# Moving one Q/K piece and the batched output rows inside a recurrent segment loop

## The chip, the cores and the metric

The kernel runs on one core of a Trainium2 chip. The metric is the device time of one execution in microseconds.

## The reference

Part A is a recurrent attention layer: 64 segments of 32 rows, each with 8 memory rows in front. The memory of the next segment is what this segment's output projection gives for those 8 rows, so the segments form one chain. Part B, a gated MLP with a spatial mix over all 2048 rows, follows and is not touched.

```python
for s in range(n_seg):                      # 64 segments, H = 32 heads of 128, Dm = 512
    h = concat([mem, x[:, 32*s:32*s+32]])   # 8 memory rows + 32 rows
    q, k, v = h @ Wq, h @ Wk, h @ Wv        # per head
    p = softmax(where(mask, q @ k.T * scale, -1e9))
    o = einsum(p @ v, Wo)                   # 40 rows x 512
    mem = o[:, :8]                          # next segment's memory
    outs.append(o[:, 8:])
# [...] residual, layer norm, part B
```

## The kernel before

An emitter records the instructions of five engines in program order and derives from read and written tokens which semaphore each one waits for. A PSUM bank is one token: a matmul that writes a bank waits until every earlier reader of that bank on another engine is done.

A matmul has 32 weight columns (`hT`, the segment's own rows) and up to 512 moving columns; four of them stand side by side in the array as four column strips. I call these four a **round**. With `held` the weights of the previous round are kept, so no load is issued. **PV** is the product of the probabilities and V, **Wo** the output projection; the matmuls of Wo come in two **stretches**. A **hole** is a time in which TensorE would only wait for another engine.

```python
    QKP = ((0, 0, 8, 0, 0), (0, 0, 8, 1, 1), (1, 0, 8, 0, 6), (1, 0, 4, 1, 7), (1, 4, 4, 1, 2))   # (head half, first, count, 0=Q 1=K, PSUM bank)
    UBK = (0, 1)
    PVB = (0, 1, 6, 7)
    VB = {(0, 0): 6, (1, 0): 7, (1, 2): 2}
    OB = 2
    XB = 3
    # [...]
    OB2 = 6
```

```python
    def QK(s, k, dc, first=0, last=3, held=False):
        b, p0, np_, mi, bank = QKP[k]
        sl = slot(s)
        ws = (w_q, w_k)[mi]
        h0, nh = 16 * b + 2 * p0, 2 * np_
        for c in range(4):
            rhs = ws[:, dc, :].rearrange("p (h c i) -> p c h i", c=4, i=32)[:, c, h0:h0 + nh, :]
            pe(lambda e, c=c, rhs=rhs: mm(e, held, ps[32 * c:32 * c + 32, bank, 0:32 * nh], hT[:, sl, dc, :], rhs,
                                          dc == first, dc == last, (0, 32 * c)),
               reads=[("hTx", (s // 4) % 3), ("hTm", s, dc // 2), ("W", mi, 2 * b), ("W", mi, 2 * b + 1)], writes=[PB(bank)])
```

Each of the five Q/K pieces is evacuated by ScalarE (L559) and then transposed by VectorE (L567). In between it lies in the buffer `Tst`, which has a place for Q and one for K, but not one for each head half: piece 2 (Q of half 1) is written over piece 0 (Q of half 0). The scores of head half 0 need pieces 0 (Q) and 1 (K); those of half 1 need pieces 2, 3 and 4.

```python
    def QK_evac(piece):
        b, p0, np_, mi, bank = piece
        st_ = Tst[:, mi, 64 * p0:64 * (p0 + np_)]
        tok = [("T", mi, k) for k in halves(b, p0, np_)]
        act(lambda e: e.activation(out=st_.rearrange("p (hp i r) -> p hp i r", i=32, r=2),
                                   in_=ps[:, bank, 0:64 * np_].rearrange("p (hp r i) -> p hp i r", r=2, i=32), func=ACT.Copy),
    # [...] VectorE transposes Tst into QT or KT
```

The recurrence runs through `mem_out`: two halves of the memory rows are transposed by small matmuls (L722) and copied into `hT`, the first by VectorE (L728), the second by ScalarE (L730).

```python
    def mem_out(s, hf):
        bank = GB[hf]
        for dd in range(2):
        # [...] small matmuls with G_sb
        dst = hT[:, slot(s + 1), 2 * hf:2 * hf + 2, 0:M]
        src = ps[:, bank, 0:2 * M].rearrange("p (dc c) -> p dc c", c=M)
        if hf == 0:
            dve(lambda e: e.tensor_copy(out=dst, in_=src), reads=[PB(bank)], writes=[("hTm", s + 1, hf)])
        else:
            act(lambda e: e.activation(out=dst, in_=src, func=ACT.Copy), reads=[PB(bank)], writes=[("hTm", s + 1, hf)])
```

The loop body, with the cuts marked. `xs` is side work for later chunks of segments; `fill` takes batched output rows (L751 and, twice per four segments, L736 and L761) from a queue: ten rounds for each four segments.

```python
        QK(s, 0, 0)
        QK(s, 1, 0, last=2, held=True)
        if s > 0:
            mem_out(s - 1, 1)
        # [...]
        QK(s, 0, 1)
        QK(s, 1, 1, last=2, held=True)
        QK(s, 0, 2)
        QK(s, 0, 3)
        QK_evac(QKP[0])
        QK(s, 1, 3, last=2, held=True)
        QK(s, 1, 2, last=2)
        QK_evac(QKP[1])
        QK(s, 2, 2, first=2, last=0, held=True)
        QK(s, 2, 3, first=2, last=0)
        QK(s, 2, 1, first=2, last=0)
        QK(s, 2, 0, first=2, last=0)
        lastop["q"] = em.by_eng["pe"][-1]
        QK_evac(QKP[2])
        QK(s, 3, 0, held=True)
        QK(s, 4, 0, last=2, held=True)
        QK(s, 3, 1)
        QK(s, 4, 1, last=2, held=True)
        QK(s, 3, 2)
        QK(s, 3, 3)
        QK_evac(QKP[3])
        QK(s, 4, 3, last=2, held=True)
        QK(s, 4, 2, last=2)
        lastop["k"] = em.by_eng["pe"][-1]
        QK_evac(QKP[4])
        # [...]
        S_half(s, 0)
        sm_exp(0)
        for dc in range(DC):
            V_half(s, 0, (0, 4), dc)            # into bank 6
        V_evac(0, "dve")
        # [...] sums, exponentials, second scores, second half of V
        nw1, nw2, nw4 = (2, 1, 2, 1)[j4], 0, 1
        # [...]
        fill(nw1)
        for f in xs[:2]:
            f()
        PV_half(s, 0)
        PV_half(s, 1)
        for f in xs[2:4]:
            f()
        fill(nw2)
        # [...] eight evacuations of PV into cT by ScalarE and VectorE
        Wo(WOQ, OB, 0, OC)
        part_evac(s, OB, 0, OC)
        Wo(WOQ[:6], OB2, OC, D)
        if s + 1 < NSEG:
            mem_out(s, 0)
            mask_dve()
        Wo(WOQ[6:], OB2, OC, D)
        cTx_copy(s)
        part_evac(s, OB2, OC, D)
        # [...]
        fill(nw4)
```

The softmax here doesn't subtract the row's maximum and nothing guards it: scores larger than these inputs give would overflow.

Of the kernel before, what the change touches and what calls it, by code (L numbers as in the profile page):

```python
# [178 lines left out]
def fast_path(nc, st, keep, A_x, A_mem0, A_Wq, A_Wk, A_Wv, A_Wo, A_seg_len, B_w_in, B_w_sp, B_b_sp, B_w_out, out):  # L179
# [98 lines left out]
    def PB(b):  # L278
        return ("ps", b)
# [4 lines left out]
    def pe(fn, **k):  # L284
        return em.add("pe", fn, **k)

    def mm(e, hold, out, lhsT, rhs, start, stop, pos):
        if not hold:
            return e.matmul(out, lhsT=lhsT, rhs=rhs, start=start, stop=stop, skip_group_check=True, tile_position=pos)  # L289
        return e.add_instruction(mybir.InstMatmult(  # L290
            name=nc.get_next_instruction_name(), engine=mybir.EngineType.PE, ins=[e.lower_ap(rhs), e.lower_ap(lhsT)], outs=[e.lower_ap(out)],
            start_tensor_calc=start, stop_tensor_calc=stop, tile_size=(128, 32), tile_position=pos, bass_skip_group_check=True,
            ldweights=False))
# [118 lines left out]
    def slot(s):  # L412
        return s % NSLOT
# [120 lines left out]
    XB = 3  # L534
    WXB = 4
    GB = (1, 2)
    OB2 = 6
    FBK = 7
    OC = 256

# [10 lines that stand above are left out]
# [4 lines left out]
# [6 lines that stand above are left out]
            reads=[PB(bank)], writes=tok)  # L561
        src = st_.bitcast(U32)
        dt_, nm = ((QT, "QT"), (KT, "KT"))[mi]
        dst = dt_[:, b, p0:p0 + np_, :, :].rearrange("p hp q r -> p (hp q r)").bitcast(U32)
        if mi == 0:
            dst = dst.rearrange("p (hp q) -> p hp q", hp=np_)[:, :, 8:40]
        dve(lambda e: e.transpose(out=dst, in_=src), reads=tok, writes=[(nm, b, k) for k in halves(b, p0, np_)])  # L567
# [16 lines left out]
    def mask_dve():  # L584
        dve(lambda e: e.tensor_copy(out=ps[:, SB, 0:448], in_=mask[:, :]), reads=["mask"], writes=[PB(SB)])
# [110 lines left out]
    def Wo(cbs, bank, d0, d1):  # L696
        for c, b in cbs:
            for g in range(4):
                h = 16 * b + 4 * c + g
                i = 8 * c + 4 * b + g  # L700
                pe(lambda e, h=h, g=g, i=i, b=b, c=c: e.matmul(  # L701
                    ps[32 * g:32 * g + 32, bank, 0:d1 - d0], lhsT=cTh[:, i, 8:40], rhs=w_o[:, h, d0:d1], start=((c, b) == WOQ[0]),
                    stop=((c, b) == WOQ[-1]), tile_position=(0, 32 * g)),
                    reads=[("cT", c, b), ("Wo", h // 8)], writes=[PB(bank)])

    def cTx_copy(s):
        j = s % 4
        dst = cTx[:, (s // 4) % 2, :, 8 * j:8 * j + 8]
        pool(lambda e: e.tensor_copy(out=dst, in_=cTh[:, :, 0:8]), reads=[("cT", c, b) for c in range(4) for b in range(2)],
             writes=[("cTx", (s // 4) % 2)])  # L710

    def part_evac(s, bank, d0, d1):
        act(lambda e: e.activation(out=part[:, s % 8, d0:d1], in_=ps[:, bank, 0:d1 - d0], func=ACT.Copy), reads=[PB(bank)],  # L713
            writes=[("part", s % 8, d0 // OC)])
# [4 lines that stand above are left out]
            dc = 2 * hf + dd  # L719
            for c in range(4):  # L720
                c0 = dc * 128 + 32 * c
                pe(lambda e, dd=dd, c=c, c0=c0: e.matmul(ps[32 * c:32 * c + 32, bank, dd * M:(dd + 1) * M], lhsT=part[:, s % 8, c0:c0 + 32],  # L722
                                                         rhs=G_sb[:, :], start=True, stop=True, skip_group_check=True, tile_position=(0, 32 * c)),
                   reads=[("part", s % 8, hf), "G"], writes=[PB(bank)])
# [6 lines that stand above are left out]
# [16 lines left out]
    def WoX_mm(rb, qr, bgs=range(8)):  # L747
        for bg in bgs:
            b, g = bg // 4, bg % 4
            h = 16 * b + 4 * qr + g  # L750
            pe(lambda e, h=h, g=g, i=8 * qr + bg: e.matmul(ps[32 * g:32 * g + 32, WXB, :], lhsT=cTx[:, rb % 2, i, :], rhs=w_o[:, h, :],  # L751
                                                           start=(i < 4), stop=(i >= H - 4), tile_position=(0, 32 * g)),
               reads=[("cTx", rb % 2), ("Wo", h // 8)], writes=[PB(WXB)])
# [181 lines left out]
    for s in range(NSEG):  # L935
        j4 = s % 4
# [9 lines left out]

        QK(s, 0, 0)
        QK(s, 1, 0, last=2, held=True)
        if s > 0:
            mem_out(s - 1, 1)  # L950
            for f in late:
                f()
        if s == NSEG - 1:
            load_h(rb)
        QK(s, 0, 1)
        QK(s, 1, 1, last=2, held=True)
        QK(s, 0, 2)
        QK(s, 0, 3)
        QK_evac(QKP[0])
        QK(s, 1, 3, last=2, held=True)  # L960
        QK(s, 1, 2, last=2)
        QK_evac(QKP[1])
        QK(s, 2, 2, first=2, last=0, held=True)
        QK(s, 2, 3, first=2, last=0)
        QK(s, 2, 1, first=2, last=0)
        QK(s, 2, 0, first=2, last=0)
        lastop["q"] = em.by_eng["pe"][-1]
        QK_evac(QKP[2])
        QK(s, 3, 0, held=True)
        QK(s, 4, 0, last=2, held=True)  # L970
        QK(s, 3, 1)
        QK(s, 4, 1, last=2, held=True)
        QK(s, 3, 2)
        QK(s, 3, 3)
        QK_evac(QKP[3])
        QK(s, 4, 3, last=2, held=True)
        QK(s, 4, 2, last=2)
        lastop["k"] = em.by_eng["pe"][-1]
        QK_evac(QKP[4])
        if s == NSEG - 1:  # L980
# [41 lines left out]
        if j4 == 0 and rb > 0:  # L1022
            assert not wq
            wq.extend(lambda rb=rb, k=k: WoX_mm(rb - 1, k // 2, range(4 * (k % 2), 4 * (k % 2) + 4)) for k in range(8))
        nw1, nw2, nw4 = (2, 1, 2, 1)[j4], 0, 1
        if not xs:
            nw1, nw2 = 1, nw1 - 1

# [24 lines left out]
# [8 lines that stand above are left out]
        if j4 == 0 and 2 <= rb + 2 < RB:  # L1061
# [904 lines left out]
def build_kernel(nc, A_x, A_mem0, A_Wq, A_Wk, A_Wv, A_Wo, A_seg_len, B_x, B_w_in, B_w_sp, B_b_sp, B_w_out, out):  # L1966
    args = (A_x, A_mem0, A_Wq, A_Wk, A_Wv, A_Wo, A_seg_len, B_w_in, B_w_sp, B_b_sp, B_w_out, out)
    with contextlib.ExitStack() as keep:
        with contextlib.ExitStack() as st:
            em, sems, dsems, flag = fast_path(nc, st, keep, *args)  # L1970
# [88 lines left out]
```

## Time and profile before

| | before |
|---|---|
| time, median of 4 runs | 854.16 us (852.58 to 854.69) |
| span of the profiled execution | 848.4 us |
| first Q/K round of segment 1, of segment 63 | 57.55, 663.69 us |
| after that (last segment and part B) | 184.7 us |
| quiet period of a segment, odd / even | 9.721 / 9.738 us |

The **period** is the distance between the first Q/K rounds (L289) of two segments (numbered from 0), read from the timeline of TensorE. Single segments are disturbed by pauses of 0.02 to 0.8 us at changing places. I therefore give the lower quartile of the periods from the fifth segment on, odd and even segments apart, and call it the quiet period; the segments differ by parity since even ones carry three batched rows and odd ones two. (In the code odd segments are those with `j4` 1 or 3.)

In a timeline line the columns are: start in us, length in us, engine, source line, operation, output and inputs, shape, count, and in brackets the idle time before it with what ended it. For TensorE the length is a modelled latency, so a pause shows as a distance between starts that is larger than the columns need: 0.216 us for a round of 512 columns, 0.109 us for 256.

### The profile page before, as it was taken

What the parts mean: (1) busy time and instruction counts of PE and PEld (TensorE: products, weight loads), DVE (VectorE), ACT (ScalarE), POOL (GpSimd) and SP (SyncE); (2) the same over time, 40 slices, a digit from 0 to 9 for tenths busy, and PEclk for the clock granted to TensorE, in tenths of its full rate; (3) what the DMA queues carried; (4) which work ended last, traced back from release to release, by engine and by line L of the source; (5) the groups of instructions that cost most, each with busy time, mean ns of one, the idle gap of its engine ahead of it and who ended that gap; (6) DMA issues with size and microseconds to landing.
All of it is one profiled execution on the core that took longest, in us unless ns stands there. A gap on an engine that the chain in (4) does not pass through costs nothing.

```text
span 848.4 us, 46072 instructions
## 1 busy us (share of the span) xinstructions
PE 834.1 (98%) x22552; PEld 438.3 (52%) x19480; DVE 515.3 (61%) x1322; ACT 471.7 (56%) x1367; POOL 168.7 (20%) x425
## 2 busy tenths in 40 slices
PE   8889999999999999999999999999999999999998
PEld 8545555555545555555555555555555544444443
DVE  3456666676666666666766666666666664453443
ACT  3446666766667676667666666767666755300000
POOL 7312212121212122221222121122111232100000
PEclk9999999999999999999999999999999999999999
DMA  9972220222332221322222324242321690033001
GB/s 319 392 231 75 69 74 28 60 72 61 77 92 58 50 66 43 75 38 61 60 73 73 95 57 80 60 94 72 58 52 56 188 280 7 1 112 106 32 12 40
DMA packets 112920, 75.25 MB, mean 89 GB/s; under 512 B 70728, under 2 KB 98512, under 8 KB 112720
## 3 DMA queue, kind: packets, MB, share of 16 engines
q1 hardware_dynamic: 111504, 70.88, 30.2%
q8 instruction: 166, 2.72, 1.3%
q0 software_dynamic: 384, 1.05, 0.3%
q10 hardware_dynamic: 832, 0.33, 0.1%
q14 instruction: 34, 0.28, 0.1%
HBM read 39.46 MB, written 20.58 MB: 71 GB/s over the span
## 4 chain that ended last, share of the span: by engine, by line
PE 92%; SPq 5%; DMA 1%; issue 0%; DVE 0%; ACT 0%
PE f_ps L289 33%; PE f_ps L701 14%; PE f_ps L290 12%; PE f_ps L1172 11%; PE f_ps L751 3%; PE f_ps L666 3%; PE f_ps L1165 3%; PE f_ps L1248 3%; SPq L329 3%; PE f_ps L1129 3%; PE f_ps L498 2%; DMA f_arena<-in_A_Wo_dram 1%; SPq L825 1%; PE f_ps L595 1%; PE f_ps L615 1%; PE f_ps L672 1%
## 5 line engine op out<-in xcount | busy, mean ns | idle before, releaser
L289 PE MATMUL f_ps<-f_arena,f_hT 128*32 128x512 bf16 (+1 forms) x5632 | 359.7, 331 | 0.3
L289 PEld LDWEIGHTS f_ps<-f_arena,f_hT 128*32 128x32 bf16 x5632 | 133.1, 96 | 161.6 <-issue 69.8
L290 PE MATMUL f_ps<-f_arena,f_hT 128*32 128x512 bf16 (+1 forms) x2560 | 188.5, 315 | 0.0
L559 ACT ACTIVATE f_Tst<-f_ps 128x512 bf16<-128x512 f32 (+1 forms) x320 | 149.7, 510 | 57.6 <-PE f_ps L289 53.9
L701 PE MATMUL f_ps<-f_arena,f_cT 128*32 128x256 bf16 x4096 | 130.6, 274 | 0.9 <-DMA f_arena<-in_A_Wo_dram 0.6
L638 POOL TENSOR_TENSOR f_E_sb<-f_R_sb,f_E_sb 128x64 bf16<-128x64 f32 x128 | 57.0, 446 | 362.1 <-ACT f_R_sb L630 362.1
L567 DVE STREAM_TRANSPOSE f_QT<-f_Tst 128x256 uint32<-128x256 uint32 x128 | 57.1, 446 | 94.3 <-ACT f_Tst L559 94.3
L701 PEld LDWEIGHTS f_ps<-f_arena,f_cT 128*32 128x32 bf16 x4096 | 90.0, 94 | 37.1 <-ACT f_cT L686 23.2
L1172 PE MATMUL f_ps<-f_arena 128*128 128x512 bf16 x448 | 100.6, 379 | 0.0
L688 DVE TENSOR_SCALAR f_cT<-f_ps 128x160 bf16<-128x160 f32 x256 | 65.2, 318 | 35.2 <-PE f_ps L672 35.2
L713 ACT ACTIVATE f_part<-f_ps 128x256 bf16<-128x256 f32 x128 | 49.1, 383 | 57.7 <-PE f_ps L701 53.7
L658 DVE TENSOR_SCALAR f_V_sb<-f_ps 128x512 bf16<-128x512 f32 (+1 forms) x128 | 71.1, 555 | 13.6 <-PE f_ps L289 13.6
L686 ACT ACTIVATE f_cT<-f_ps 128x160 bf16<-128x160 f32 x256 | 57.1, 310 | 36.3 <-PE f_ps L672 36.3
L1172 PEld LDWEIGHTS f_ps<-f_arena 128*128 128x128 bf16 x448 | 43.8, 98 | 52.8
L567 DVE STREAM_TRANSPOSE f_KT<-f_Tst 128x128 uint32<-128x128 uint32 (+1 forms) x192 | 65.9, 356 | 2.8
L626 ACT ACTIVATE f_R_sb<-f_ps 128x160 f32<-128x160 f32 x128 | 38.9, 304 | 34.8 <-PE f_ps L290 34.8
L634 DVE TENSOR_TENSOR f_E_sb<-f_R_sb,f_E_sb 128x160 bf16<-128x160 f32 x128 | 41.7, 326 | 23.4 <-ACT f_R_sb L630 23.4
L1178 DVE TENSOR_TENSOR f_arena<-f_ps,f_arena 128x512 f32<-128x512 f32 x28 | 19.3, 690 | 54.4 <-PE f_ps L1172 52.4
L289 PE MATMUL f_ps<-f_arena,f_hTe 128*32 128x512 bf16 x640 | 48.8, 382 | 0.0
L608 ACT ACTIVATE f_E_sb<-f_ps 128x224 bf16<-128x224 f32 x128 | 45.9, 359 | 0.1
L751 PE MATMUL f_ps<-f_arena,f_cTx 128*32 128x512 bf16 x512 | 43.9, 379 | 0.5 <-issue 0.4
L630 ACT ACTIVATE f_R_sb<-f_R_sb 128x160 f32<-128x160 f32 x128 | 42.6, 332 | 2.0
(123 smaller groups left out, 1027.3 us busy)
## 6 DMA issues: line engine op xcount, KB each, us to landing
wT_d<-f_wst SPq DMA_DIRECT2D x32, 256.0 KB
f_arena<-wT_d SPq DMA_DIRECT2D x32, 256.0 KB
f_arena<-in_A_Wv_dram SPq DMA_DIRECT2D x4, 1024.0 KB
f_arena<-in_A_Wk_dram SPq DMA_DIRECT2D x4, 1024.0 KB
f_arena<-in_A_Wo_dram SPq DMA_DIRECT2D x4, 1024.0 KB
f_Vx<-vext_d SPq DMA_DIRECT2D x124, 32.0 KB
f_arena<-in_A_Wq_dram SPq DMA_DIRECT2D x3, 1024.0 KB
vext_d<-f_Vs SPq DMA_DIRECT2D x20, 128.0 KB
```

The lines of the kernel that those rows point to most:

```text
L289: return e.matmul(out, lhsT=lhsT, rhs=rhs, start=start, stop=stop, skip_group_check=True, tile_position=pos)
L290: return e.add_instruction(mybir.InstMatmult(name=nc.get_next_instruction_name(), engine=mybir.EngineType.PE, ins=[e.lower_ap(rhs), e.lowe ...
L559: act(lambda e: e.activation(out=st_.rearrange("p (hp i r) -> p hp i r", i=32, r=2), in_=ps[:, bank, 0:64 * np_].rearrange("p (hp r i) -> ...
L567: dve(lambda e: e.transpose(out=dst, in_=src), reads=tok, writes=[(nm, b, k) for k in halves(b, p0, np_)])
L638: pool(lambda e: e.tensor_tensor(out=ev, in0=rv, in1=ev, op=ALU.mult), reads=[("R", b), ("Ex", b)], writes=[("Ex", b)])
L658: dve(lambda e: e.tensor_scalar(out=dst, in0=src, scalar1=VSC, scalar2=None, op0=ALU.mult), reads=[PB(bank)], writes=tok)
L686: act(lambda e: e.activation(out=dst, in_=src, func=ACT.Copy, scale=UNSC), reads=[PB(PVB[c])], writes=tok)
L688: dve(lambda e: e.tensor_scalar(out=dst, in0=src, scalar1=UNSC, scalar2=None, op0=ALU.mult), reads=[PB(PVB[c])], writes=tok)
L701: pe(lambda e, h=h, g=g, i=i, b=b, c=c: e.matmul(ps[32 * g:32 * g + 32, bank, 0:d1 - d0], lhsT=cTh[:, i, 8:40], rhs=w_o[:, h, d0:d1], star ...
L713: act(lambda e: e.activation(out=part[:, s % 8, d0:d1], in_=ps[:, bank, 0:d1 - d0], func=ACT.Copy), reads=[PB(bank)], writes=[("part", s % ...
L751: pe(lambda e, h=h, g=g, i=8 * qr + bg: e.matmul(ps[32 * g:32 * g + 32, WXB, :], lhsT=cTx[:, rb % 2, i, :], rhs=w_o[:, h, :], start=(i < 4 ...
L1172: pe(lambda e: e.matmul(ps[:, bank, 0:TB], lhsT=z2[:, sc, fb * 128:(fb + 1) * 128], rhs=wTb[tb % 2][:, :, sc, :], start=(sc == 0), stop=(s ...
```

## The change

The intent: the first two blocks of piece 2 go ahead, one before the second memory half and one after it, so that TensorE has more to do while that half travels from the Wo stretch into `hT`. Since that work takes the place of the batched row behind the Wo stretch, the rows go to places around PV. The second Wo stretch moves to bank 7 so that piece 2 can use bank 6 early. Rounds that load weights fall from 12 to 10 of 20.

```diff
--- before.py
+++ after.py
@@ -534,7 +534,7 @@
     XB = 3
     WXB = 4
     GB = (1, 2)
-    OB2 = 6
+    OB2 = 7
     FBK = 7
     OC = 256
 
@@ -946,6 +946,7 @@
 
         QK(s, 0, 0)
         QK(s, 1, 0, last=2, held=True)
+        QK(s, 2, 0, last=3, held=True)
         if s > 0:
             mem_out(s - 1, 1)
             for f in late:
@@ -954,27 +955,26 @@
             load_h(rb)
         QK(s, 0, 1)
         QK(s, 1, 1, last=2, held=True)
+        QK(s, 2, 1, last=3, held=True)
         QK(s, 0, 2)
         QK(s, 0, 3)
         QK_evac(QKP[0])
         QK(s, 1, 3, last=2, held=True)
         QK(s, 1, 2, last=2)
         QK_evac(QKP[1])
-        QK(s, 2, 2, first=2, last=0, held=True)
-        QK(s, 2, 3, first=2, last=0)
-        QK(s, 2, 1, first=2, last=0)
-        QK(s, 2, 0, first=2, last=0)
+        QK(s, 2, 2, held=True)
+        QK(s, 2, 3)
         lastop["q"] = em.by_eng["pe"][-1]
         QK_evac(QKP[2])
-        QK(s, 3, 0, held=True)
-        QK(s, 4, 0, last=2, held=True)
-        QK(s, 3, 1)
-        QK(s, 4, 1, last=2, held=True)
-        QK(s, 3, 2)
-        QK(s, 3, 3)
+        QK(s, 3, 3, first=3, last=0, held=True)
+        QK(s, 4, 3, first=3, last=2, held=True)
+        QK(s, 3, 1, first=3, last=0)
+        QK(s, 4, 1, first=3, last=2, held=True)
+        QK(s, 3, 2, first=3, last=0)
+        QK(s, 3, 0, first=3, last=0)
         QK_evac(QKP[3])
-        QK(s, 4, 3, last=2, held=True)
-        QK(s, 4, 2, last=2)
+        QK(s, 4, 0, first=3, last=2, held=True)
+        QK(s, 4, 2, first=3, last=2)
         lastop["k"] = em.by_eng["pe"][-1]
         QK_evac(QKP[4])
         if s == NSEG - 1:
@@ -1022,7 +1022,7 @@
         if j4 == 0 and rb > 0:
             assert not wq
             wq.extend(lambda rb=rb, k=k: WoX_mm(rb - 1, k // 2, range(4 * (k % 2), 4 * (k % 2) + 4)) for k in range(8))
-        nw1, nw2, nw4 = (2, 1, 2, 1)[j4], 0, 1
+        nw1, nw2, nw4 = 2, (1, 0, 1, 0)[j4], 0
         if not xs:
             nw1, nw2 = 1, nw1 - 1
```

## The prediction

> **What bounds the kernel now.** I read the page first, then the timeline of single segments, because the page misleads here.
>
> ```profile
> PE 834.1 (98%) x22552; PEld 438.3 (52%) x19480; DVE 515.3 (61%) x1322; ACT 471.7 (56%) x1367; POOL 168.7 (20%) x425
> ...
> PE 92%; SPq 5%; DMA 1%; issue 0%; DVE 0%; ACT 0%
> ```
>
> By these lines TensorE is full. But each matmul is drawn for its latency (379 ns for 512 columns), while the next round of four 32-column strips starts 0.216 us after it (109 ns at 256 columns). A pause of up to 0.16 us after a 512-column round is invisible as idle time, so I read start-to-start distances. The 64 recurrent segments lie between about 47 and 674 us. In quiet ones the first Q/K round (L289) recurs every 9.72 to 9.74 us, although the stretch carries two batched-row rounds (L751, L736, L761) in segments 1 and 3 of each four, three in 0 and 2, and none in the first four segments: those, too, take 9.72 us. Two rounds, 0.43 us of work, change nothing: the segment is a chain of latencies, and the rows fill holes in it. What matters is which hole each row leaves and which it enters.
>
> The boundary, PE timeline. First segment 1 to 2, without any batched row:
>
> ```profile
> 66.82 0.39 PE L701 MATMUL f_ps<-f_arena,f_cT 128*32 128x256 bf16 x8
> 67.27 0.40 PE L289 MATMUL f_ps<-f_arena,f_hT 128*32 128x512 bf16 x4
> ```
>
> Then segment 36 to 37, with a row behind the Wo stretch:
>
> ```profile
> 408.29 0.39 PE L701 MATMUL f_ps<-f_arena,f_cT 128*32 128x256 bf16 x8
> 408.50 0.39 PE L751 MATMUL f_ps<-f_arena,f_cTx 128*32 128x512 bf16 x4
> 408.74 0.40 PE L289 MATMUL f_ps<-f_arena,f_hT 128*32 128x512 bf16 x4
> 408.96 0.39 PE L290 MATMUL f_ps<-f_arena,f_hT 128*32 128x512 bf16 x4
> 409.18 0.20 PE L722 MATMUL f_ps<-f_G_sb,f_part 128*32 128x8 bf16 x8
> ```
>
> From the last two Wo rounds to the first Q/K round it is 0.45 us **with the row and without**. Two Wo rounds are 0.22; the other 0.23 is the row, or a pause. The pin is the first memory half: VectorE copies it into hT (L728) from 408.51 to 408.68, and L289 follows 0.05 later.
>
> The Q/K evacuation, ScalarE, VectorE and TensorE timelines of segment 37:
>
> ```profile
> 410.36 1.08 ACT L559 ACTIVATE f_Tst<-f_ps 128x512 bf16<-128x512 f32 x2 [0.72 <-PE f_ps L289]
> 411.65 1.31 ACT L559 ACTIVATE f_Tst<-f_ps 128x512 bf16<-128x512 f32 x3 [0.21 <-PE f_ps L289]
> 412.85 0.37 ACT L608 ACTIVATE f_E_sb<-f_ps 128x224 bf16<-128x224 f32 x1
> ```
>
> ```profile
> 410.99 0.45 DVE L567 STREAM_TRANSPOSE f_QT<-f_Tst 128x256 uint32<-128x256 uint32 x1 [0.82 <-ACT f_Tst L559]
> 411.48 0.45 DVE L567 STREAM_TRANSPOSE f_KT<-f_Tst 128x256 uint32<-128x256 uint32 x1
> ```
>
> ```profile
> 412.30 0.27 PE L595 MATMUL f_ps<-f_QT,f_KT 128*32 128x40 bf16 x16
> ```
>
> Pieces 0 and 1 of Q/K are ready for the scores (L595) at 411.92; the scores start at 412.30: **0.38 us of slack** that the page does not show.
>
> PV, PE timeline: segment 37 (one row ahead of PV), then 36 (two rows):
>
> ```profile
> 414.54 0.39 PE L751 MATMUL f_ps<-f_arena,f_cTx 128*32 128x512 bf16 x4
> 414.75 0.61 PE L498 MATMUL f_ps<-f_arena,f_hTe 128*32 128x512 bf16 x8
> 415.29 0.27 PE L666 MATMUL f_ps<-f_E_sb,f_V_sb 32*128 32x40 bf16 x16
> 415.41 0.19 PE L672 MATMUL f_ps<-f_E_sb,f_Vx 32*128 32x64 bf16 x4
> 415.62 0.27 PE L666 MATMUL f_ps<-f_E_sb,f_V_sb 32*128 32x40 bf16 x16
> 415.79 0.21 PE L672 MATMUL f_ps<-f_E_sb,f_Vx 32*128 32x64 bf16 x4
> ```
>
> ```profile
> 405.89 0.20 PE L672 MATMUL f_ps<-f_E_sb,f_Vx 32*128 32x64 bf16 x4
> 405.92 0.28 PE L666 MATMUL f_ps<-f_E_sb,f_V_sb 32*128 32x40 bf16 x16
> 406.05 0.21 PE L672 MATMUL f_ps<-f_E_sb,f_Vx 32*128 32x64 bf16 x4
> 406.19 0.61 PE L498 MATMUL f_ps<-f_arena,f_hTe 128*32 128x512 bf16 x8
> 406.65 0.51 PE L701 MATMUL f_ps<-f_arena,f_cT 128*32 128x256 bf16 x12
> ```
>
> With one row the second half waits from 415.41 to 415.62, 0.19 more than the 0.03 that the four small matmuls need; with two it follows after 0.03.
>
> **What the Trainium skill says.** "TensorE: Matmul & The Clock Gate", section "Back-to-back issue gap", gives N/2.4 + 2.5 ns warm: 216 and 109 ns for 512 and 256 columns, as this trace has them. The same page, Part 2, says that the queue pulls weight loads ahead of running matmuls; the trace agrees: rounds with a load (L289) and rounds that keep the weights (L290) are both 0.216 apart. "TensorEngine Tiling (Array Packing)", "Key Properties", says that changing the tiling mode drains TensorE; either side of PV 0.11 us is lost in every segment, and the change does not touch it. "Perfetto Trace Analysis", "Identifying the Most-Contended Engine", says that matmul busy time is a poor measure; the 98% above is an example.
>
> **The change part by part.**
>
> *Weights.* Rounds of Q/K that load weights fall from 12 to 10 of 20, 8 loads per segment. As both kinds take 0.216, this is worth 0.
>
> *Row out of the boundary.* QK start stays pinned by the first memory half, so removing the row leaves a pause of 0.23, as in the first segments. Gain 0.
>
> *Two rounds of piece 2 early.* One goes between the first and second memory half, one before the third block. Today a pause of about 0.03 plus 0.01 stands at the third block (409.45 to 409.69 is 0.247 for one round). The second half's chain (transpose 409.18, copied by ScalarE 409.46 to 409.64) moves 0.216 later with its matmuls but gets 0.216 more cover behind it. The pause goes: -0.045. Q/K is then 12 rounds of 0.216, 8 of 0.109 and 0.054 for L722, some 3.52 us, and TensorE reaches the scores at 412.26.
>
> *But piece 0 ends two rounds later*, less the pause. Its last round starts at 410.31 instead of 409.92. ScalarE starts 0.44 after such a start (409.92 to 410.36), so at 410.75. Back to back the large evacuations start 0.49 apart (1.08 minus 0.59 for one), so piece 1 goes 411.24 to 411.83; VectorE follows 0.03 after and needs 0.45: K is ready at 412.31, and the scores start about 0.055 later at **412.37**. Against 412.30 that is +0.065: the slack of 0.38 is eaten and the 0.045 with it. Behind it, piece 2 follows at 411.74, pieces 3 and 4 at 412.27 and 412.55, the exponential at 412.81 (before: 412.85), so ScalarE does not add. The last K transpose ends at 413.40, and the second scores stand at 413.46: just fits. The softmax chain hangs on the first sums, so it moves by +0.065 as a whole.
>
> *Rows around PV, segments 1 and 3.* nw1 goes from 1 to 2: PE would reach the last four matmuls of PV at 415.75, but GpSimd's product holds them at 415.785 anyway. Cost 0 to 0.015.
>
> *Rows around PV, segments 0 and 2.* nw1 stays at 2, one row enters behind PV. There are two other rounds there already, and Wo starts 0.03 after they end. The row pushes Wo by 0.216 - 0.03, and some 0.02 of small pauses for cT in Wo disappear: +0.167. From Wo the chain to the boundary has a fixed length (last round of the first Wo stretch, evacuation 0.38, transpose, copy 0.17: 1.29 us), so this is all on the path.
>
> *OB2 from bank 6 to 7.* It only frees bank 6 for the early rounds. The first Wo stretch has already waited for the last reader of 7. Cost 0.
>
> **Sum.** 30 segments x (0.065 + 0.007) = 2.2 us; 30 x (0.065 + 0.167) = 7.0 us; the first four segments 4 x 0.065 = 0.3 us. Together +9.4 us; 853.65 + 9.4 = **863.0 us**, 1.1% more. The stages outside the loop are unchanged.
>
> **The rivals.** (1) *The second memory half is the real bound and the rows are free around PV.* For it speaks the pause of 0.045 at the third block, and the free rows of the first segments. Against it: the 0.45 us at the boundary with or without a row, and no hole behind PV. It would make 63 x -0.045 = -3 us: 851. (2) *TensorE throughput is the bound*, as 98% suggests: work is conserved, so 853 to 854. Against it stand equal periods with 0 and 2 rows. (3) *ScalarE and VectorE become the bound* in the compressed Q/K evacuation: the second scores have a margin of only 0.01, and if they slip 0.05 to 0.1 more, 64 segments add 3 to 6 us: 866 to 869. For it: five evacuations and five transposes now stand in one run.
>
> **Range and chances.** The row behind PV (7 us with its shift) is the surest term by the trace; the scores' wait rests on an estimated sequence and may be 0 to 0.12. That gives 858 to 868. Leaving something for rival 1, I take 857 to 869. Slower by over 2% would need 871, some 0.27 us in each segment: 0.06. Faster by over 2% has nothing to come from: 0.01. Within 2%: 0.93.
>
> **What would show it.** In the changed profile: no L751 between L701 and L289, and a start-to-start of 0.45 there; no pause ahead of the third block; L595 starting 3.63 us after the first Q/K round instead of 3.57, waiting for the KT transpose; the second PV half behind the first with no 0.19 pause in any later segment; Wo some 0.8 us after the last PV matmuls in segments 0 and 2 (0.60 today); periods of 9.80 (1, 3) and 9.97 (0, 2). The prediction is wrong if the boundary closes to 0.22, or if L595 follows Q/K unpaused.

## The result

The changed kernel took 865.63 us (863.77 to 868.57, 4 runs) against 854.16 us. The ratio is 1.0141, with a 95% interval of 1.0109 to 1.0173: slower by 1.4%. A ratio here is the mean time of one kernel's fast runs over that of the other's fast runs of the same rounds, so it is not quite the ratio of the medians quoted. Five more runs later gave 865.54 against 852.37 us, ratio 1.0162 (1.0141 to 1.0183). Results are correct.

The quiet periods are 9.881 us (odd) and 10.039 us (even), which is +0.160 and +0.301. With +0.143 in the first four segments, which carry no rows, that makes 30 x 0.160 + 30 x 0.301 + 4 x 0.143 = +14.4 us. The rest after the loop is unchanged (184.8 us). With medians instead of lower quartiles the differences are +0.162 and +0.280 and the sum is +13.8 us, since about half of the even segments before stand near 9.76 rather than 9.738.

The page of the changed kernel, its first line of busy times:

```profile
PE 846.3 (98%) x22552; PEld 440.4 (51%) x18968; DVE 505.1 (58%) x1322; ACT 465.0 (54%) x1367; POOL 168.6 (20%) x425
```

TensorE still shows 98% and the same 22552 matmuls, but 12 us more busy time. The new pauses are counted as busy, for they hide under modelled latencies. The 512 weight loads that went are visible (19480 to 18968); no gain from them shows.

The boundary of segments 36 and 37 in the timeline of TensorE:

```profile
417.99 0.39 PE L701 MATMUL f_ps<-f_arena,f_cT 128*32 128x256 bf16 x8
418.44 0.40 PE L289 MATMUL f_ps<-f_arena,f_hT 128*32 128x512 bf16 x4
```

There is no row any more between the last two Wo rounds and the first Q/K round, and it is still 0.45 us. The hole of 0.23 us is now empty.

The third block of Q/K, in the kernel before and then in the changed one:

```profile
409.45 0.39 PE L290 MATMUL f_ps<-f_arena,f_hT 128*32 128x512 bf16 x4
409.69 0.61 PE L289 MATMUL f_ps<-f_arena,f_hT 128*32 128x512 bf16 x8
```

```profile
419.37 0.60 PE L290 MATMUL f_ps<-f_arena,f_hT 128*32 128x512 bf16 x8
419.80 0.60 PE L289 MATMUL f_ps<-f_arena,f_hT 128*32 128x512 bf16 x8
```

Two rounds take 0.43 now: the pause that stood here (0.247 for one round) is gone, as intended. What it was exchanged for shows on ScalarE and VectorE, and then on TensorE. The first ScalarE line covers all five evacuations; the next two, each from a narrower window, are the second (piece 1) and the third (piece 2) alone:

```profile
420.45 2.32 ACT L559 ACTIVATE f_Tst<-f_ps 128x512 bf16<-128x512 f32 x5 [0.89 <-PE f_ps L289]
```

```profile
420.95 0.59 ACT L559 ACTIVATE f_Tst<-f_ps 128x512 bf16<-128x512 f32 x1
```

```profile
421.62 0.60 ACT L559 ACTIVATE f_Tst<-f_ps 128x512 bf16<-128x512 f32 x1
```

```profile
421.08 0.45 DVE L567 STREAM_TRANSPOSE f_QT<-f_Tst 128x256 uint32<-128x256 uint32 x1 [1.21 <-ACT f_Tst L559]
421.57 0.45 DVE L567 STREAM_TRANSPOSE f_KT<-f_Tst 128x256 uint32<-128x256 uint32 x1
```

```profile
421.86 0.28 PE L289 MATMUL f_ps<-f_arena,f_hT 128*32 128x256 bf16 x4
422.07 0.28 PE L595 MATMUL f_ps<-f_QT,f_KT 128*32 128x40 bf16 x16
422.19 0.20 PE L601 MATMUL f_ps<-f_QT,f_arena 128*32 128x64 bf16 x4
422.27 1.05 PE L289 MATMUL f_ps<-f_arena,f_hT 128*32 128x512 bf16 x16
```

Before, the five evacuations came in two groups with a pause of 0.21 between them; now they are one run, but for 0.08 ahead of the third. The KT transpose ends at 421.57 + 0.45 = 422.02, and the scores start at 422.07, 0.21 after a Q/K round that needs 0.11. So the scores wait 0.11, and start 3.63 us after the first Q/K round (3.57 before).

**A second wait stands behind the scores.** From L601 to V's first round (L289) it is 0.086 us; in segment 37 of the kernel before it was 0.030:

```profile
412.41 0.20 PE L601 MATMUL f_ps<-f_QT,f_arena 128*32 128x64 bf16 x4
412.44 1.03 PE L289 MATMUL f_ps<-f_arena,f_hT 128*32 128x512 bf16 x16
```

V's first half is written to bank 6, which piece 2 holds until its evacuation ends, at 421.62 + 0.60 = 422.22; V starts 0.05 later. The prediction had not seen this. The first round after such a wait also takes 0.226 instead of 0.215, so it costs 0.067 in all.

Piece 2's evacuation is itself late. The first two evacuations start 0.50 apart (420.45, 420.95), the third only 0.67 after the second. It needs the place of piece 0 in `Tst` (which has a place for Q and one for K, but not one for each head half), and VectorE's transpose of piece 0 ends at 421.08 + 0.45 = 421.53; the evacuation starts 0.09 later. That distance is 0.09 in nearly all segments of every run with this order (0.22 in the kernel before), and the semaphore that comes last ahead of this evacuation is VectorE's.

The wait totals name the first of the two waits, that of the scores, directly (engine, line, what it waited for: us in total, times, longest). These are idle times of the weight loads, longer than what TensorE loses:

```profile
PEld f_ps L595 <- DVE f_KT L567: 14.2, 64, 0.7
```

Before, this wait occurred once in the whole execution; now it occurs in all 64 segments.

PV and Wo, timeline of TensorE, segment 37 and then segment 38 (even):

```profile
425.47 0.20 PE L672 MATMUL f_ps<-f_E_sb,f_Vx 32*128 32x64 bf16 x4
425.50 0.29 PE L666 MATMUL f_ps<-f_E_sb,f_V_sb 32*128 32x40 bf16 x16
425.63 0.21 PE L672 MATMUL f_ps<-f_E_sb,f_Vx 32*128 32x64 bf16 x4
425.77 0.61 PE L498 MATMUL f_ps<-f_arena,f_hTe 128*32 128x512 bf16 x8
426.24 1.73 PE L701 MATMUL f_ps<-f_arena,f_cT 128*32 128x256 bf16 x56
```

```profile
435.51 0.21 PE L672 MATMUL f_ps<-f_E_sb,f_Vx 32*128 32x64 bf16 x4
435.65 0.61 PE L498 MATMUL f_ps<-f_arena,f_hTe 128*32 128x512 bf16 x8
436.09 0.39 PE L751 MATMUL f_ps<-f_arena,f_cTx 128*32 128x512 bf16 x4
436.31 1.70 PE L701 MATMUL f_ps<-f_arena,f_cT 128*32 128x256 bf16 x56
```

In segment 37 the second PV half follows the first after 0.03 us, where it took 0.21: the row ahead of PV has filled that hole. In segment 38 the row behind PV puts Wo 0.80 us after PV's last matmuls instead of 0.60.

### The profile page after: what moved, and what is told of

It reads as the page before. It is cut to its first block, busy times and chain, and to the rows that moved or that the text cites. A ratio compares the mean times of both kernels' runs of the same rounds, so it can differ in the third digit from the quotient of the medians.

```text
span 864.1 us, 45545 instructions
## 1 busy us (share of the span) xinstructions
PE 846.3 (98%) x22552; PEld 440.4 (51%) x18968; DVE 505.1 (58%) x1322; ACT 465.0 (54%) x1367; POOL 168.6 (20%) x425
## 4 chain that ended last, share of the span: by engine, by line
PE 90%; DMA 3%; SPq 3%; DVE 2%; issue 1%; ACT 1%; ACTq 0%
PE f_ps L289 30%; PE f_ps L290 15%; PE f_ps L701 12%; PE f_ps L1172 11%; PE f_ps L751 3%; PE f_ps L1165 3%; PE f_ps L1248 3%; PE f_ps L666 2%; PE f_ps L595 2%; PE f_ps L1129 2%; SPq L329 2%; PE f_ps L498 2%; DMA f_arena<-in_A_Wk_dram 2%; PE f_ps L615 1%; DVE f_hT L728 1%
## 5 line engine op out<-in xcount | busy, mean ns | idle before, releaser
L289 PE MATMUL f_ps<-f_arena,f_hT 128*32 128x512 bf16 (+1 forms) x5120 | 334.7, 327 | 4.0 <-ACT f_Tst L559 0.2
L289 PEld LDWEIGHTS f_ps<-f_arena,f_hT 128*32 128x32 bf16 x5120 | 124.8, 96 | 159.6 <-issue 70.2
L559 ACT ACTIVATE f_Tst<-f_ps 128x512 bf16<-128x512 f32 (+1 forms) x320 | 143.1, 509 | 57.2 <-PE f_ps L289 51.6
L701 PEld LDWEIGHTS f_ps<-f_arena,f_cT 128*32 128x32 bf16 x4096 | 97.9, 96 | 28.7 <-ACT f_cT L686 14.7
L1172 PE MATMUL f_ps<-f_arena 128*128 128x512 bf16 x448 | 100.6, 379 | 0.0
L1172 PEld LDWEIGHTS f_ps<-f_arena 128*128 128x128 bf16 x448 | 43.7, 98 | 52.8
L567 DVE STREAM_TRANSPOSE f_KT<-f_Tst 128x128 uint32<-128x128 uint32 (+1 forms) x192 | 60.3, 340 | 2.8
L289 PE MATMUL f_ps<-f_arena,f_hTe 128*32 128x512 bf16 x640 | 49.0, 382 | 0.0
L751 PE MATMUL f_ps<-f_arena,f_cTx 128*32 128x512 bf16 x512 | 41.2, 379 | 0.0
```

Source lines behind the costliest of these rows:

```text
L289: return e.matmul(out, lhsT=lhsT, rhs=rhs, start=start, stop=stop, skip_group_check=True, tile_position=pos)
L567: dve(lambda e: e.transpose(out=dst, in_=src), reads=tok, writes=[(nm, b, k) for k in halves(b, p0, np_)])
L701: pe(lambda e, h=h, g=g, i=i, b=b, c=c: e.matmul(ps[32 * g:32 * g + 32, bank, 0:d1 - d0], lhsT=cTh[:, i, 8:40], rhs=w_o[:, h, d0:d1], star ...
L751: pe(lambda e, h=h, g=g, i=8 * qr + bg: e.matmul(ps[32 * g:32 * g + 32, WXB, :], lhsT=cTx[:, rb % 2, i, :], rhs=w_o[:, h, :], start=(i < 4 ...
L1172: pe(lambda e: e.matmul(ps[:, bank, 0:TB], lhsT=z2[:, sc, fb * 128:(fb + 1) * 128], rhs=wTb[tb % 2][:, :, sc, :], start=(sc == 0), stop=(s ...
```

## The experiments

The theory after the result: a segment is a chain of latencies with holes of known sizes. The change takes a row out of a hole (boundary), puts it into another hole in odd segments (+0.02) and on the path in even ones (+0.16), and its Q/K order makes the scores wait for the evacuation chain and V for bank 6 (+0.14 in each segment). The rivals: TensorE's work is the bound; or the second memory half is the bound and the rows alone cost. "Quiet sum" below is what the quiet periods add up to over the loop, computed as above.

| run | ratio (95%) | quiet period odd / even | quiet sum |
|---|---|---|---|
| before | 1 | 9.721 / 9.738 | 0 |
| the change, first and second time | 1.0141, 1.0162 | 9.881 / 10.039 | +14.4 us |
| 1 order alone | 1.0108 (1.0087 to 1.0129) | 9.863 / 9.879 | +9.1 |
| 2 rows alone | 1.0042 (1.0022 to 1.0062) | 9.738 / 9.900 | +5.4 |
| 3 odd rows alone | 1.0011 (0.9990 to 1.0032) | 9.738 / 9.738 | +0.5 |
| 4 change, piece 2 in bank 3 | 1.0111 (1.0089 to 1.0133) | 9.816 / 9.975 | +10.3 |
| 5 as 4, rows back | 1.0098 (1.0081 to 1.0116), again 1.0064 (1.0046 to 1.0083) | 9.800 / 9.817 | +5.0 |
| 6 second block early alone | 0.9982 (0.9964 to 0.9999), again 0.9991 (0.9970 to 1.0013) | 9.678 / 9.696 | -2.7 |
| 7 first block early alone | 1.0008 (0.9991 to 1.0024) | 9.725 / 9.741 | +0.2 |
| 8 two rows behind Wo | 1.0108 (1.0084 to 1.0131) | 9.908 / 9.908 | +10.7 |

### 1. The order alone

```diff
# the changed kernel, with
-        nw1, nw2, nw4 = 2, (1, 0, 1, 0)[j4], 0
+        nw1, nw2, nw4 = (2, 1, 2, 1)[j4], 0, 1
```

> The changed kernel with the batched rows back where they were (only the Q/K order and the bank of the second Wo stretch changed). My theory: two pauses come from the order alone, the scores' wait for the KT transpose (+0.065 us against before, net of the removed pause of 0.045) and the wait of V's first round for bank 6, which piece 2 now leaves later (+0.07, seen only in the changed kernel's trace). So each of 64 segments is 0.135 longer, quiet periods 9.86 (odd) and 9.875 (even), time 854.2 + 8.6 = 862.8 us. Rival (the second memory half was the bound, the order helps and only the rows cost): 851 us and no pause ahead of L595.

Measured: 861.99 us against 852.18, ratio 1.0108, some 9.2 us. The quiet periods are 0.142 longer in odd and 0.141 in even segments, against 0.135 expected. The order alone makes the kernel slower, and the rows are not needed for it; the rival is out.

### 2. The rows alone

```diff
# the kernel before, with
-        nw1, nw2, nw4 = (2, 1, 2, 1)[j4], 0, 1
+        nw1, nw2, nw4 = 2, (1, 0, 1, 0)[j4], 0
```

> The kernel before with only the batched rows moved (nw line of the change). My theory: the boundary stays 0.45 us from the last two Wo rounds to the first Q/K round, now with a pause of 0.23 in it; odd segments stay within 0.015 of 9.72, even ones grow by 0.167 to about 9.91: 30 x 0.167 + 30 x 0.007 = +5.2, time 859.4 us. Rival (rows are free around PV and cost behind Wo): 60 x 0.216 less, about 841 us; rival (TensorE work conserved): 854 us.

Measured: 856.15 us, ratio 1.0042, some 3.6 us. The periods are +0.017 in odd and +0.162 in even segments (expected up to 0.015, and 0.167). The boundary in the timeline of TensorE:

```profile
420.62 0.39 PE L701 MATMUL f_ps<-f_arena,f_cT 128*32 128x256 bf16 x8
421.07 0.40 PE L289 MATMUL f_ps<-f_arena,f_hT 128*32 128x512 bf16 x4
```

It is 0.45 us without the row, as with it. Both rivals are out, for the interval lies above 1. The quiet sums of experiments 1 and 2 add up to 14.5, against 14.4 for the whole change: no interaction of the two parts shows.

### 3. The rows of odd segments alone

```diff
# the kernel before, with
-        nw1, nw2, nw4 = (2, 1, 2, 1)[j4], 0, 1
+        nw1, nw2, nw4 = 2, 0, (1, 0, 1, 0)[j4]
```

> The kernel before with the row moved only in segments 1 and 3 of each four: one more row ahead of PV, none behind Wo; segments 0 and 2 as before. My theory: one hole for another, the row ahead of PV fills the 0.19 wait of the second PV half and the boundary pauses 0.23 instead: odd periods 9.72 to 9.735, time 854.2 to 854.7 us. Rival (a row behind Wo is on the path): 30 x 0.216 = 6.5 us less, 848 us. Rival (a row ahead of PV is on the path): 6 us more, 860 us.

Measured: 854.04 us against 852.18, ratio 1.0011; odd periods 9.738, even ones unchanged. Moving a row of 0.216 us of TensorE time from one hole to another costs 0.017. Neither rival's 6 us shows, in either direction.

### 4. Piece 2 in bank 3

```diff
# the changed kernel, with piece 2 = (1, 0, 8, 0, bank)
-(1, 0, 8, 0, 6)
+(1, 0, 8, 0, 3)
```

> The changed kernel with piece 2 of Q/K in PSUM bank 3, which the side work has left by then, instead of bank 6, which V's first half takes next. My theory: V's first round no longer waits for the evacuation of piece 2, 0.07 us less in each segment: 865.6 - 4.5 = 861.1 us; the pause after the scores (L601 to L289, 0.086) falls to 0.03 and the one ahead of L595 (0.216 for a 256-column round) stays. Rival (V waits for something else, such as the exponential or the scores' drain): no change, 865.6 us.

Measured: ratio 1.0111, against 1.0141 and 1.0162 for the change itself in other rounds. The intervals of 1.0111 and 1.0141 overlap, so what follows rests on the periods and the trace. The quiet periods fall by 0.065 and 0.064, where 0.07 was expected. The timeline of TensorE:

```profile
421.19 0.28 PE L289 MATMUL f_ps<-f_arena,f_hT 128*32 128x256 bf16 x4
421.40 0.28 PE L595 MATMUL f_ps<-f_QT,f_KT 128*32 128x40 bf16 x16
421.52 0.20 PE L601 MATMUL f_ps<-f_QT,f_arena 128*32 128x64 bf16 x4
421.55 1.03 PE L289 MATMUL f_ps<-f_arena,f_hT 128*32 128x512 bf16 x16
```

L601 to L289 is back to 0.03, while the scores' wait (0.21 ahead of L595) stays. So V did wait for bank 6, and for nothing else of that length. Piece 2's evacuation is as late as before (0.09 after the transpose of piece 0); with another bank it no longer matters to V.

### 5. Piece 2 in bank 3 and the rows back

The edits of experiments 1 and 4 together, run twice.

> The changed kernel with both piece 2 in bank 3 and the batched rows back. My theory: of the change only the scores' wait for the KT transpose is left, +0.065 net: quiet odd periods 9.79, ratio to before 1.005 (+4 us). Rival (bank 6 was the whole cost of the order): ratio 0.997, since then the removed pause of 0.045 would be a gain.

> The same kernel as e5_order_bank3_rows_back, whose quiet periods (9.80 and 9.82) sum to +5 us while its four runs gave +8. If the periods tell the whole of it, the ratio is 1.006 (1.004 to 1.008); if something outside the quiet segments costs 3 us, it is 1.010 again.

Measured: ratio 1.0098 from four runs and, again, 1.0064 from six. The quiet periods are +0.079 the first time and +0.082 the second. The first set is 3 us above what its periods say, the second is not; the difference is not in the quiet segments, and what disturbed three of the four runs stays open. What both show is that the scores' wait alone makes the kernel slower than before: the removed pause is not worth it. It costs more than the 0.06 by which the scores start later: their first matmuls after the wait also take 0.115 instead of 0.104 us (L595 to L601).

### 6. Only the second block early

```diff
# the kernel before, with
         QK(s, 1, 1, last=2, held=True)
+        QK(s, 2, 1, first=1, last=0, held=True)
         QK(s, 0, 2)
# [...]
-        QK(s, 2, 2, first=2, last=0, held=True)
-        QK(s, 2, 3, first=2, last=0)
-        QK(s, 2, 1, first=2, last=0)
-        QK(s, 2, 0, first=2, last=0)
+        QK(s, 2, 2, first=1, last=0, held=True)
+        QK(s, 2, 3, first=1, last=0)
+        QK(s, 2, 0, first=1, last=0)
```

> The kernel before with one block of piece 2 early, the second one, between the second memory half and the third block; rows and banks as before. My theory: the extra round covers the pause at the third block (0.045), piece 0 is only one round later and the scores have 0.38 of slack, so L595 follows Q/K unpaused and V's bank 6 is free in time: each period 0.045 shorter, 9.68 odd; ratio 0.9966, some 2.9 us less, faster than both kernels. Rival (any early block costs through the evacuation chain): ratio 1.002 or more. Rival (the segment is held by something else): ratio 1.000.

> The same kernel as e6_one_block_early, whose quiet periods (9.68 and 9.70) sum to -2.7 us and whose runs gave 0.9982 (0.9964 to 0.9999). Expected: ratio 0.997 (0.995 to 0.999).

Measured: 850.10 us against 852.13, ratio 0.9982, and again 851.36 against 852.37, ratio 0.9991. The quiet periods are 0.043 and 0.042 shorter, and again 0.040 and 0.043, as expected (0.045). The timeline of TensorE:

```profile
409.63 0.60 PE L290 MATMUL f_ps<-f_arena,f_hT 128*32 128x512 bf16 x8
410.06 0.39 PE L289 MATMUL f_ps<-f_arena,f_hT 128*32 128x512 bf16 x4
...
412.34 0.28 PE L289 MATMUL f_ps<-f_arena,f_hT 128*32 128x256 bf16 x4
412.45 0.27 PE L595 MATMUL f_ps<-f_QT,f_KT 128*32 128x40 bf16 x16
412.55 0.20 PE L601 MATMUL f_ps<-f_QT,f_arena 128*32 128x64 bf16 x4
412.58 0.60 PE L289 MATMUL f_ps<-f_arena,f_hT 128*32 128x512 bf16 x8
```

The pause at the third block is gone (two rounds in 0.43), the scores follow Q/K after 0.11, and V follows the scores after 0.03. This is the good part of the change without its costs. Its medians are the lowest in their rounds, but the gain over before is small: by the periods 2.7 us, by the runs 1 to 2 us, and the second interval includes 1.

### 7. Only the first block early

The first block of piece 2 goes ahead of the second memory half, the second Wo stretch to bank 7; K's first blocks are swapped so that each held round follows its weights.

```diff
# the kernel before, with
-    OB2 = 6
+    OB2 = 7
         QK(s, 1, 0, last=2, held=True)
+        QK(s, 2, 0, last=1, held=True)
# [...]
-        QK(s, 2, 2, first=2, last=0, held=True)
-        QK(s, 2, 3, first=2, last=0)
-        QK(s, 2, 1, first=2, last=0)
-        QK(s, 2, 0, first=2, last=0)
+        QK(s, 2, 2, last=1, held=True)
+        QK(s, 2, 3, last=1)
+        QK(s, 2, 1, last=1)
# [...] pieces 3 and 4: blocks in the order 1, 0, 2, 3
```

> The kernel before with one block of piece 2 early, the first one, ahead of the second memory half, and the second Wo stretch in bank 7 as the change has it; rows as before. My theory: the half's transpose moves back with the round, so the pause of some 0.03 to 0.045 at the third block stays; nothing else waits: quiet odd periods 9.72, ratio 1.000. Rival (the block ahead of the half is what covers it): ratio 0.9966, periods 9.68. Rival (bank 7 for the second Wo stretch costs): periods longer.

Measured: ratio 1.0008; periods 9.725 and 9.741. In the timeline of TensorE the pause at the third block is still there, 0.25 for one round:

```profile
411.30 0.39 PE L290 MATMUL f_ps<-f_arena,f_hT 128*32 128x512 bf16 x4
411.55 0.61 PE L289 MATMUL f_ps<-f_arena,f_hT 128*32 128x512 bf16 x8
```

A block ahead of the half's transpose delays that transpose by as much as it covers. Of the two early blocks only the one after the half does the covering. No cost of bank 7 for the second Wo stretch shows (+0.003 to +0.004).

### 8. Two rows behind Wo

```diff
# the kernel before, with
-        nw1, nw2, nw4 = (2, 1, 2, 1)[j4], 0, 1
+        nw1, nw2, nw4 = (1, 0, 1, 0)[j4], 0, 2
```

> The kernel before with two rows behind the Wo stretch and one fewer ahead of PV. My theory: the hole at the boundary is 0.23 and holds one row; the second is on the path, +0.216, while taking it from ahead of PV gives nothing back (the second PV half waits instead): quiet periods 9.94 odd and even, 60 x 0.21 = +12.6 us, ratio 1.0147. Rival (rows are just work, wherever they stand): ratio 1.000.

Measured: ratio 1.0108; periods 9.908 in both parities, +0.187 and +0.170, where 9.94 was expected. The boundary in the timeline of TensorE:

```profile
424.91 0.39 PE L701 MATMUL f_ps<-f_arena,f_cT 128*32 128x256 bf16 x8
425.13 0.60 PE L751 MATMUL f_ps<-f_arena,f_cTx 128*32 128x512 bf16 x8
425.56 0.39 PE L289 MATMUL f_ps<-f_arena,f_hT 128*32 128x512 bf16 x4
```

The hole at the boundary holds one row: with a second one Q/K starts at 0.65 instead of 0.45. That is 0.20 rather than 0.216, for the second row first uses up the 0.02 that one row leaves free; I had overlooked that, and the 0.01 that the first round after a wait takes longer. The amount of work is the same as before, so a bound by TensorE's work is excluded.

### 9. The change once more

> The changed kernel once more, to stand beside the next two on one chip. The quiet periods of its trace (9.88 and 10.04 against 9.72 and 9.74) sum to +14.4 us over 64 segments; its four runs gave +11.5 to 12. Expected: ratio 1.013 to 1.017.

Measured: ratio 1.0162 (1.0141 to 1.0183), periods 9.880 and 10.038, as in the first trace.

## Why the prediction was right

The time lay inside the range, at 865.6 for 863.0. The boundary, the scores' wait and the rows came out as worked out; one wait of 4.3 us was missed. That it fell inside is in part luck: the range left 6 us upward for an inexact scores' wait, and not for a second wait. Point by point:

- **The boundary is pinned by the first memory half.** Right: 0.45 us in the changed kernel and in experiment 2, and one row fits (experiment 8).
- **The early rounds remove the pause at the third block.** Right as a sum. Experiments 6 and 7 show that only the second of the two rounds does it; the prediction left open which.
- **The scores wait for piece 1 through ScalarE and VectorE.** Right: 3.63 us after the first Q/K round, as worked out; +0.06 measured for +0.065. In all it cost some 0.08 (experiment 5). The wait stays when the bank is changed (experiment 4) and goes when only one round is ahead (experiment 6).
- **"Piece 2 follows at 411.74 [...] so ScalarE does not add."** This step was wrong, in two places. The sequence let piece 2 follow piece 1 back to back, 3.00 us after the first Q/K round. It came at 3.18, for it has to wait until piece 0 is transposed out of `Tst`. The exponential behind it came at 4.21 instead of 4.07; nothing on TensorE waited for that, and the second scores held. And the prediction did not ask which matmul needs the PSUM bank that an evacuation frees: V needs bank 6. Expected 0, measured 0.067 in each segment, 4.3 us over the loop, shown by experiment 4 (-0.065). Both are needed: by an estimate from these numbers, an evacuation at 3.00 would have freed bank 6 at about 3.65, and without the bank V starts at 3.77 (experiment 4). The part of `Tst` is read from the code and the trace; no run gave piece 2 a place of its own.
- **Rows in odd segments, 0 to 0.015.** Measured 0.017 (experiment 3).
- **Row behind PV in even segments, 0.167.** Measured 0.162 (experiment 2).
- **Weights and bank 7, 0.** Nothing shows; experiment 7 has bank 7, 256 loads fewer (19224) and periods within 0.004.
- **Small readings.** The wait of the second PV half is 0.18, not 0.19 (0.21 less 0.03). The slack of 0.38 includes some 0.055 that pass between a transpose and the scores in any case; the sum for the scores had these in it.

With the missed term the sum is 9.4 + 4.3 = 13.7 us, against 14.4 by the quiet periods; the rest is the order alone at 0.142 rather than 0.065 + 0.067 (60 x 0.010 = 0.6, about the 0.011 of the slower first scores), odd rows at 0.017 rather than 0.007 (0.3) and even rows at 0.162 rather than 0.167 (-0.15). The runs themselves gave 11.5 (difference of the medians, first time) and 13.2 (second time). The disturbed segments make up 2 to 6 us per profile and differ from run to run; whether a slower loop absorbs a part of them was not tested and stays open.

Of the rivals, the first fails by experiment 1 (the order alone is slower) and experiment 2 (rows around PV are not free); its pause at the second memory half was real, though, and worth 0.043 (experiment 6). TensorE's work as the bound is refuted by experiments 1, 2 and 8, which do the same matmuls in 9.2, 3.6 and 9.2 us more. The third, ScalarE and VectorE as a new bound, was partly true: not at the second scores, where it was looked for, but at bank 6.

## What to carry to other kernels

In a loop that is a chain of latencies, measure each hole by the distance between starts, and move filler work only between holes; here work taken out of a hole gained nothing, and the same work outside a hole cost most of its length (0.16 to 0.19 of 0.216). When matmuls are put ahead of an evacuated result, follow the result to everything that waits for it: its consumers, and also the next writer of each buffer that it passes through. Of two moves that are meant to cover the same wait, only the one behind the start of the waiting chain covered it here, so try each one alone.

## What the Trainium skill lacked or had wrong

- "TensorE: Matmul & The Clock Gate", "Back-to-back issue gap", gives a sustained 131 ns per matmul of 512 columns in a real stream of loads and matmuls. Here the 448 full-array matmuls of part B (L1172), each with its own load, are 216 ns apart within a group, and so are the four-strip rounds of Q/K with a load and without one. That is the page's own isolated gap.
- "Perfetto Trace Analysis", "Identifying the Most-Contended Engine", warns of matmul busy time for the roofline, but not that pauses are hidden in it. Here the same 22552 matmuls show 834.1 us and 846.3 us of busy time, both 98%, because pauses of up to 0.16 us behind a 512-column round count as busy.
- "TensorEngine Tiling (Array Packing)", "Key Properties", says that a change of tiling mode drains TensorE, but gives no cost. The pause either side of PV, which I put down to it without isolating it, was 0.11 us in most segments of both kernels, and never under 0.08.
- "Perfetto Trace Analysis", "Matmuls", advises to rotate banks between matmul groups. It does not say that the order of evacuations decides when a bank is free: with piece 2 and V in bank 6 the changed order cost 0.067 us in each segment.
- No page that I used has the cost of a hand-over from VectorE or ScalarE to the engine that waits: 0.03 us from ScalarE to VectorE, 0.09 from VectorE to ScalarE, and 0.05 from either to the next matmul.
